# Releasing the Q, K and V loads of later batches one attention unit at a time, and moving two other loads to another DMA queue

## The chip, the cores and the metric

The kernel runs on one core of a Trainium2 chip. The metric is the device time of one execution in microseconds (us). On the chips used here the kernel before varied from 345 to 350 us in nearly all of its runs, so differences under 1% are not read as effects.

## The reference, cut to what matters

```python
# attention: 8 batches, 8 heads, 576 positions, head size 64, window of 32 on each side
scores = scale * q @ k.T ;  masked outside |i - j| <= 32 ;  softmax ;  x = attn @ v
# then, on all 4608 tokens (x is 4608 x 512):
h = x @ w_in                  # 512 -> 2048
g = s * max(h, 0)**2 + b      # s and b are two scalars
out = g @ w_out               # 2048 -> 512
```

## The kernel before

The kernel is written as a list of tasks. Each has an engine, a function, an assumed duration, and what it reads and writes. A small scheduler in Python orders the tasks per engine by simulating them with the assumed durations, including the DMA transfers. On the chip, each engine then executes its own list strictly in that order and waits on semaphores. So an assumed duration is never waited for. It only decides the order, and an engine whose next instruction is not ready stands still even if a later one is ready.

The parts that matter here, with cuts marked `...`:

```python
add("pool", [lambda e: e.dma_start(SB128[:, 0:1], moe_s.partition_broadcast(128)),      # s, b by GpSimd
             lambda e: e.dma_start(SB128[:, 1:2], moe_b.partition_broadcast(128))], ...)

def load_v(b, h, key, stream, waits=()):      # V of one head -> VST; stream is the issuing engine
    ...
def cast_v(b, key, engines, slack):           # VST (f32) -> VBD (bf16), on VectorE and ScalarE
    ...
def chunk(b, t0, n, key):                     # one of three pieces of Q and of K, b >= 2
    for name in "qk":
        add("sp", ... dma_start(STG ...),
            waits=[land["av", b - 1, {0: int(b > 3), 256: 2, 512: 3}[t0]]], ...)
        add("dve", ... NAT <- STG ...)        # cast
        add("sp", ... QT or KT <- NAT, transpose=True ...)
    ...
def unit(b, m):                               # one of five attention units of a batch
    ...   # scores, exp, AV, normalise; XT <- XN by a DMA transpose from SP for b >= 2
    land["av", b, m] = g.tasks[-1]            # the AV matmuls: what later loads wait for
...
# batch 1
    w_out(0); qk(1, 0, 128)
    for h in range(H):
        load_v(1, h, nxt(), "pool", waits=[land["out", 2, 0]])
    cast_v(1, due(1, 0) - 4.0, (("dve", "act"), ("dve", "act")), 800.0)
...
# batches 2 to 7
    for h in range(H):
        load_v(b, h, due(b, 0) - 30.0 + 0.1 * h, "pool", waits=[land["av", b - 1, 1]])
```

`land["av", b - 1, u]` is the end of the AV matmuls of unit `u` of the batch before. VST is a single buffer, filled in 8 pieces of 144 KB for batches 0 and 1, and 16 of 72 KB later. Plain loads, the DMA transposes of xt, Q and K, and the output DMAs are all issued by SP. V of batches 1 to 7 and the scalars are issued by GpSimd (POOL).

The softmax here doesn't subtract the row's maximum and nothing guards it: scores larger than these inputs give would overflow.

## Time and profile before

The median was 347.02 us (346.45 to 349.16, three runs). The profiled run spans 345.8 us.

First, lines of the profile page of the kernel before: busy time with its share of the span, and then the span in 40 equal slices, with busy tenths, the granted TensorE clock in tenths and the DMA share in tenths.

```profile
PE 311.9 (90%) x2234; PEld 178.4 (52%) x2234; DVE 208.0 (60%) x485; ACT 167.2 (48%) x270; POOL 95.5 (28%) x146
...
PE   1587948997999998799979998999999999999995
...
PEclk9999987999999999899999999999999999999999
DMA  6999996799799699936994799569942111110021
```

TensorE (PE) is busy 90% of the time and is the bound. DMA is saturated for the first 50 us, then comes in bursts. The clock drops twice, each time behind a gap in the PE row.

The windows view of the kernel before gives, for each stretch, its length and then PE, PEld, DVE, ACT and POOL busy with their counts, the granted clock, the DMA share and GB/s.

```profile
0.00:20.00 20.00, 7.58 (x62) 5.33 (x62) 11.95 (x28) 12.92 (x16) 13.96 (x29) 1.00 0.94 209
20.00:40.00 20.00, 16.59 (x236) 14.19 (x237) 11.37 (x25) 13.08 (x25) 9.18 (x11) 1.00 1.07 346
40.00:60.00 20.00, 13.96 (x152) 11.74 (x151) 11.85 (x18) 10.97 (x17) 11.90 (x12) 0.83 0.96 228
60.00:80.00 20.00, 20.00 (x228) 16.92 (x226) 10.11 (x23) 10.09 (x21) 10.58 (x17) 1.00 0.93 201
80.00:130.00 50.00, 48.23 (x356) 27.34 (x355) 41.09 (x105) 30.18 (x49) 18.29 (x29) 1.00 0.94 187
130.00:180.00 50.00, 44.83 (x270) 22.50 (x269) 31.95 (x76) 22.73 (x36) 11.70 (x20) 0.97 0.94 183
```

The idle time of TensorE in a stretch is its length less PE busy: 12.4 us in the first 20 us, 6.0 us between 40 and 60, 5.2 us between 130 and 180. The clock of 0.83 over 20 us stands for 6.8 us at half rate. The same view with narrower stretches:

```profile
49.70:53.40 3.70, 0.00 (x0) 0.00 (x0) 3.01 (x6) 2.15 (x4) 0.00 (x0) 0.50 1.12 278
53.40:56.60 3.20, 3.20 (x18) 2.28 (x19) 3.20 (x6) 1.82 (x2) 2.63 (x2) 0.51 1.02 336
141.90:145.30 3.40, 3.40 (x10) 1.22 (x8) 3.40 (x6) 1.30 (x3) 0.00 (x0) 0.50 1.16 233
```

The view of waits for PE of the kernel before has who waited for whom, the total, how often, and the longest.

```profile
...
PE o L715 <- DVE gt L705: 5.8, 1, 5.8
PE w L696 <- DMA xt<-xn: 4.3, 2, 2.2
PE o L474 <- DVE nat L470: 2.9, 1, 2.9
...
PE o L715 <- DVE outs L728: 1.6, 1, 1.6
```

The 5.8 us are at 47.6 to 53.4 us, the 4.3 us are two waits for transposes of xt between 130 and 180 us, and the 2.9 us are in the startup. The timelines of VectorE and GpSimd show what lies behind the first one (start, duration, engine, line, operation; in brackets the idle time before it and what ended it).

```profile
50.39 1.42 DVE L447 CAST vbd<-vst 64x1024 bf16<-64x1024 f32 x2 [5.86 <-DMA vst<-in_v_dram]
...
36.96 5.89 POOL L433 DMA_DIRECT2D vst<-in_v_dram  x8 [0.73 <-DMA stg<-in_moe_w_out_dram]
48.65 1.04 POOL L466 CAST nat<-stg 128x1024 bf16<-128x1024 f32 x1 [3.21 <-DMA stg<-in_q_dram]
53.91 1.68 POOL L466 CAST nat<-stg 32x1024 bf16<-32x1024 f32 x1 [4.22 <-DMA stg<-in_q_dram]
```

VectorE stands 5.86 us in front of the cast of V of batch 1, and the gt tile that TensorE wants comes after that cast in VectorE's list.

### The profile page before, as it was taken

How to read it: one execution, taken by the hardware profiler on the slowest of the kernel's cores; microseconds unless marked ns; L12 is line 12 of the kernel's file. 1: busy time of each engine (PE TensorE's matmuls, PEld its weight loads, DVE VectorE, ACT ScalarE, POOL GpSimd, SP SyncE). 2: the span in 40 equal slices, each digit the busy share in tenths (PEclk: the TensorE clock that was granted, in tenths of full speed). 3: DMA queues.
4: the chain of work that ended last, by engine and by line, in shares of the span. 5: the costliest groups of instructions: out<-in, count | busy, mean ns of one | idle time of the engine just before them, and what ended most of it. 6: DMA issues, size and time to landing. Idle time of an engine off the chain costs nothing.

```text
span 345.8 us, 5858 instructions
## 1 busy us (share of the span) xinstructions
PE 311.9 (90%) x2234; PEld 178.4 (52%) x2234; DVE 208.0 (60%) x485; ACT 167.2 (48%) x270; POOL 95.5 (28%) x146
## 2 busy tenths in 40 slices
PE   1587948997999998799979998999999999999995
PEld 0456846884564564255535554555455544444442
DVE  6565538646985984587567666964984453333321
ACT  6596537635662763365337446544654433333300
POOL 7652836470290082006400640074000000000000
PEclk9999987999999999899999999999999999999999
DMA  6999996799799699936994799569942111110021
GB/s 189 219 342 363 264 226 209 191 226 193 168 245 204 152 166 210 217 106 165 230 196 121 189 209 220 151 162 231 223 105 76 47 46 44 40 51 32 30 78 75
DMA packets 103388, 57.15 MB, mean 165 GB/s; under 512 B 51776, under 2 KB 95424, under 8 KB 103360
## 3 DMA queue, kind: packets, MB, share of 16 engines
q1 hardware_dynamic: 98176, 48.51, 61.0%
q0 software_dynamic: 5184, 8.27, 12.2%
q8 instruction: 17, 0.28, 0.3%
q14 instruction: 11, 0.09, 0.1%
HBM read 36.70 MB, written 9.44 MB: 133 GB/s over the span
## 4 chain that ended last, share of the span: by engine, by line
PE 58%; DMA 28%; SPq 5%; DVE 3%; POOL 3%; issue 1%; ACT 0%; DVEq 0%; POOLq 0%
PE o L715 25%; PE w L696 25%; DMA xt<-xn 10%; DMA stg<-in_k_dram 7%; DMA vst<-in_v_dram 5%; PE avn L583 4%; DMA stg<-in_moe_w_in_dram 3%; PE sc L544 3%; DMA stg<-in_q_dram 3%; SPq L433 3%; POOL vst L433 3%; SPq L457 1%; SPq L417 1%; DVE vbd L447 1%; DVE nat L507 1%
## 5 line engine op out<-in xcount | busy, mean ns | idle before, releaser
L715 PE MATMUL o<-wout,gt 128*128 128x512 bf16 (+1 forms) x640 | 143.5, 359 | 7.8 <-DVE gt L705 5.8
L696 PE MATMUL w<-xt,win 128*128 128x512 bf16 (+2 forms) x704 | 145.7, 344 | 4.3 <-DMA xt<-xn 4.3
L703 ACT ACTIVATE r<-w 128x512 bf16<-128x512 f32 x144 | 85.6, 597 | 104.9 <-PE w L696 91.7
L433 POOL DMA_DIRECT2D vst<-in_v_dram x104 | 65.9, 641 | 117.3 <-PE avn L583 111.5
L705 DVE TENSOR_TENSOR gt<-r 128x512 bf16<-128x512 bf16 x144 | 62.2, 438 | 57.3 <-ACT r L703 56.7
L715 PEld LDWEIGHTS o<-wout,gt 128*128 128x128 bf16 x640 | 61.2, 98 | 66.6 <-DVE gt L705 6.3
L696 PEld LDWEIGHTS w<-xt,win 128*128 128x128 bf16 x704 | 62.1, 99 | 58.0 <-DMA xt<-xn 5.2
L728 DVE SCALAR_TENSOR_TENSOR outs<-o,sb,cvec 128x512 f32<-128x512 f32 (+1 forms) x40 | 27.7, 692 | 17.1 <-PE o L715 17.0
L561 ACT ACTIVATE exe<-sc 128x512 bf16<-128x512 f32 (+1 forms) x40 | 27.6, 690 | 11.9 <-PE sc L544 11.8
L583 PE MATMUL avn<-vbd,exo 128*128 128x130 bf16 (+1 forms) x240 | 27.7, 220 | 4.5 <-ACT xt L608 2.2
L596 DVE TENSOR_TENSOR xn<-avn,rec 128x512 bf16<-128x512 f32 (+1 forms) x38 | 26.1, 686 | 9.1 <-DMA xt<-xn 8.5
L446 ACT CAST vbd<-vst 64x1024 bf16<-64x1024 f32 (+1 forms) x15 | 16.6, 1140 | 24.2 <-DMA vst<-in_v_dram 24.2
L507 DVE CAST nat<-stg 128x1024 bf16<-128x1024 f32 (+1 forms) x36 | 24.2, 683 | 4.0 <-DMA stg<-in_q_dram 2.8
L583 PEld LDWEIGHTS avn<-vbd,exo 128*128 128x128 bf16 (+1 forms) x240 | 21.7, 104 | 9.2 <-ACT xt L608 2.4
L583 PE MATMUL avn<-vbd,exe 128*128 128x130 bf16 (+1 forms) x152 | 25.1, 219 | 0.5 <-ACT vbd L446 0.5
L561 ACT ACTIVATE exo<-sc 128x512 bf16<-128x512 f32 x32 | 23.7, 741 | 3.4 <-PE sc L544 3.4
L544 PEld LDWEIGHTS sc<-qt,kbd 128*128 128x128 bf16 x288 | 20.3, 100 | 9.6 <-issue 0.9
L544 PE MATMUL sc<-qt,kbd 128*128 128x128 bf16 (+1 forms) x288 | 24.7, 220 | 0.1
L447 DVE CAST vbd<-vst 64x1024 bf16<-64x1024 f32 (+1 forms) x16 | 11.6, 747 | 14.6 <-DMA vst<-in_v_dram 14.6
L522 DVE COPY kbd<-kt 64x512 bf16<-64x512 bf16 (+1 forms) x72 | 18.3, 254 | 0.9
L583 PEld LDWEIGHTS avn<-vbd,exe 128*128 128x128 bf16 (+1 forms) x152 | 16.0, 108 | 3.6 <-ACT vbd L446 0.6
L565 DVE TENSOR_TENSOR exe<-exe,mask 128x512 bf16<-128x512 bf16 (+1 forms) x30 | 11.8, 392 | 5.9 <-ACT exe L561 5.4
(65 smaller groups left out, 135.6 us busy)
## 6 DMA issues: line engine op xcount, KB each, us to landing
stg<-in_q_dram SPq DMA_DIRECT2D x16, 512.0 KB, 5.1
stg<-in_k_dram SPq DMA_DIRECT2D x16, 512.0 KB, 8.3
out_dram<-outs SPq DMA_DIRECT2D x32, 256.0 KB, 2.2
vst<-in_v_dram POOLq DMA_DIRECT2D x96, 72.0 KB, 7.4
stg<-in_moe_w_in_dram SPq DMA_DIRECT2D x8, 512.0 KB, 9.2
stg<-in_moe_w_out_dram SPq DMA_DIRECT2D x8, 512.0 KB, 11.2
vst<-in_v_dram SPq DMA_DIRECT2D x8, 144.0 KB, 4.6
vst<-in_v_dram POOLq DMA_DIRECT2D x8, 144.0 KB, 8.4
```

What stands on the lines that cost most here:

```text
L433: add(stream, lambda e, dst=dst, src=src: e.dma_start(dst, src), 640.0 if stream == "sp" else 700.0, writes=[("VST", h, x) for x in (range ...
L507: add("dve", lambda e, si=si, ni=ni: e.tensor_copy(NAT[ni][0:n, :, :].rearrange("p i (h d) -> p h i d", h=H), STG[si][0:n, 0:1024].rearran ...
L522: add("dve", lambda e, i=i, p0=p0: e.tensor_copy(KBD[p0:p0 + 64, :, j0:j0 + nj, p0 + 32 * i:p0 + 32 * i + 32], KT[p0:p0 + 64, i, :, t0 // ...
L544: fns = [lambda e, j=j, pr=pr, lo=lo, hi=hi, w=w, par=par: e.matmul(SC[:, par, pr * 128:pr * 128 + w], lhsT=KBD[:, pr, j, :], rhs=QT[slot] ...
L561: add("act", lambda e, src=src, dst=dst: e.activation(dst.rearrange("p a (c i) -> p a i c", i=2), src, AF.Exp, bias=0.0, scale=0.125), 190 ...
L583: fns.append(lambda e, pr=pr, buf=buf, col=col, j=j, x=x, last=len(parts) - 1: e.matmul(av[0:nr, pr, 0:130], lhsT=buf[:, pr, col:col + nr] ...
L596: add("dve", lambda e: e.tensor_tensor(XN[xi][0:nr, :].rearrange("p (a b c) -> p a b c", a=4, b=2), av[0:nr, :, 0:128].rearrange("p a (b c ...
L696: add("pe", [lambda e, g=g, kc=kc: e.matmul(wt[:, g, :], lhsT=WIN_BF[:, kc, (f0 + g) * 128:(f0 + g + 1) * 128], rhs=XT[:, kc, t0 % XR:t0 % ...
L703: add("act", lambda e: e.activation(rt, wt, AF.Relu, bias=0.0, scale=1.0), 190 + 0.833 * 512, reads=[("W", wb)], writes=[("R1", rb)], key=key)
L705: add("dve", lambda e: e.tensor_tensor(GT[gs][:, f0:f0 + ng, g0:g0 + nt], rt, rt, ALU.mult), 130 + 0.53 * 512, reads=[("R1", rb)], writes= ...
L715: add("pe", [lambda e, fc=fc: e.matmul(O[:, ob, 0:cn], lhsT=GT[gs][:, fc, g0:g0 + 128], rhs=WOUT_BF[:, fc, c0:c0 + cn], start=(fc == 0), s ...
L728: add("dve", lambda e: e.scalar_tensor_tensor(OUTS[us][:, 0:cn], O[:, ob, 0:cn], SB128[:, 0:1], CVEC[:, c0:c0 + cn], ALU.mult, ALU.add), 2 ...
```

## The change

The intent: load V of batch 1 and the two scalars through SP; let each Q, K and V piece of batches 2 to 7 follow its own attention unit of the batch before, instead of several following one unit; and bring the scheduler's assumed durations nearer to measured ones. The core of the diff:

```diff
+XTS = 4000.0
+PACE = ((0, 0, 1, 2, 3, 3), (0, 0, 1, 2, 3, 3), (0, 1, 2, 3, 3, 3))
+PACEV = ((0, 0, 1, 1), (0, 0, 1, 1), (0, 1, 2, 2))
-        add("pool", [lambda e: e.dma_start(SB128[:, 0:1], moe_s.partition_broadcast(128)),
-                     lambda e: e.dma_start(SB128[:, 1:2], moe_b.partition_broadcast(128))], ...
+            for i, src in enumerate((moe_s, moe_b)):          # after the w_in loads
+                add("sp", lambda e, i=i, src=src: e.dma_start(SB128[:, i:i + 1], src.partition_broadcast(128)), ...
-                load_v(1, h, nxt(), "pool", waits=[land["out", 2, 0]])
+                load_v(1, h, nxt(), "sp", waits=[land["out", 2, 0]])
-                    load_v(b, h, due(b, 0) - 30.0 + 0.1 * h, "pool", waits=[land["av", b - 1, 1]])
+                    load_v(b, h, due(b, 0) - 30.0 + 0.1 * h, "pool", waits=[land["av", b - 1, PACEV[min(b, 4) - 2][h // 2]]])
-                    waits=[land["av", b - 1, {0: int(b > 3), 256: 2, 512: 3}[t0]]], dma=("l", n // 2, 28.5))
+                    waits=[land["av", b - 1, PACE[min(b, 4) - 2][t0 // 128 + "qk".index(name)]]], dma=("l", n // 2, 30.0))
 # assumed durations (they only order the instructions); two lines that sum up seven edits
-  w_out DMA 46.0, weight casts dve 650 / pool 1500, V DMA pool 230 / sp 20, Q K DMA 27.4, Q cast pool 1400
+  w_out DMA 48.0, weight casts dve 690 / pool 1100, V DMA pool 370 / sp 21, Q K DMA 30.0, Q cast pool 1150
-                writes=[("W", wb)], key=key, slack=1500.0)    # first matmuls behind a DMA transpose
+                writes=[("W", wb)], key=key, slack=XTS)
```

No arithmetic and no bytes change. Because the scheduler reruns, the order of the instructions on every engine changes too.

## The prediction

> **What bounds the kernel now.** TensorE does. The page's busy table has PE at 311.9 of 345.8 us. The windows view (10 us stretches) places the 34 us of idle: about 20 us before 40 us, where inputs and weights arrive (DMA share 1.05 to 1.13); 6.0 us between 40 and 60; about 8.3 us between 80 and 250; then none until the last few microseconds. After 250 us PE never stops. Two steps of the granted clock go with the stalls: the 50 to 60 us window has 0.67 and the 140 to 150 us window 0.83, which cost about 3.3 and 1.7 us. This fits the Trainium skill, "TensorE: Matmul & The Clock Gate", Part 1: an idle array falls to half rate. So about 19 us sit in stalls after 40 us.
>
> **What they are.**
> 1. 47.6 to 53.4 us: PE waits 5.84 us for a gt tile of VectorE. In the timeline, VectorE stands in order behind the cast of V of batch 1, which waits 5.86 us until V lands at 50.4. GpSimd issued that V from 37.0 to 42.8 (734 ns each, 8.4 us median to landing), into a saturated DMA system.
> 2. 83 us: PE waits 1.6 us behind VectorE, which waited for V of batch 2 (16 issues, 65.4 to 75.4; last landing at 81.2).
> 3. 130 to 180 us: PE waits 2.2 and 2.0 us for DMA transposes of xt, which took about 9 us where the median is 2.6. All 16 V pieces are released by one attention unit and issued in 10 us among Q and K pieces of 512 KB: DMA share 1.1 to 1.2, then 0.2 to 0.6.
> 4. 211 and 246 us: 0.9 and 0.4 us behind K loads that took 12 to 14 us.
>
> **What the change does.** No arithmetic and no bytes change. The second batch's V goes from the GpSimd queue into SP's, in order with the Q, K loads. An SP issue of V took 1.17 us for batch 0 (8 in 9.34 us), so it costs SP about 3 us more, but V no longer shares with Q and K pieces issued after it. I estimate its landing at 48 to 49 us instead of 50.4, and the later Q, K about 2 us later. The s and b loads leave GpSimd (1.3 us, not critical). In the steady part V is released by two or three units in turn, and Q and K one unit apart: bursts become a flatter load, so transposes and K loads should lose most of their waiting. The larger assumed DMA times and the 4.0 us allowance behind transposes order consumers later.
>
> **Sum.** Stall 1 with its clock loss: 9.2 us, of which I expect 5 (what follows it is still fed by DMA; new waits for Q or K appear). Stall 2: 1 of 1.6. Stalls 3 and 4 with the clock loss and small gaps: 4 of 8. Startup: 0. About 9.5 us less: 337.5 us, range 332 to 344. Faster by over 2%: 0.72; within: 0.25; slower: 0.03.
>
> **What would show it.** PE idle from 40 to 60 us below 3 us, and a clock near 1.0 there; no xt wait over 1 us between 130 and 180; peak DMA share nearer 1.0; PE busy near 307 us (less half-rate time); the idle before 40 us and the tail unchanged.
>
> **What would make it wrong.** VectorE still blocks on V of batch 1, as SP's slow issue lands it later than the schedule believes; SP's in-order waits for attention units hold up the transposes and outputs behind them; or the new order of instructions opens stalls in the startup.

## The result, and the profile after

| | before | after |
|---|---|---|
| time, median (range), 4 runs each | 348.09 us (346.45 to 349.35) | 333.11 us (331.69 to 334.12) |
| ratio, 95% interval | | 0.9569 (0.9508 to 0.963) |
| span of the profiled run | 345.8 us | 331.1 us |
| TensorE busy | 311.9 us | 308.5 us |

Ratios here are the mean time of one kernel's fast runs over that of the other's in the same rounds, so not quite the ratio of the medians quoted.

The profile page of the kernel after, the same rows:

```profile
PE 308.5 (93%) x2199; PEld 179.5 (54%) x2234; DVE 206.6 (62%) x485; ACT 166.4 (50%) x270; POOL 87.6 (26%) x136
...
PE   1778998899999999999989999999999999999995
...
PEclk9999999799999999999999999999999999999999
DMA  8999999899999699979998996999811111000021
```

Most of the holes in the middle of the PE row are gone. The windows view of the kernel after:

```profile
0.00:20.00 20.00, 9.50 (x80) 6.86 (x82) 11.87 (x29) 14.45 (x19) 14.50 (x28) 1.00 1.07 238
20.00:40.00 20.00, 17.60 (x252) 16.04 (x250) 12.96 (x27) 12.86 (x24) 7.19 (x7) 1.00 1.10 343
40.00:60.00 20.00, 17.76 (x212) 15.35 (x213) 11.57 (x24) 15.35 (x28) 8.36 (x9) 1.00 1.11 254
60.00:80.00 20.00, 18.84 (x172) 14.38 (x171) 12.38 (x27) 9.05 (x15) 8.17 (x14) 0.92 0.95 213
80.00:130.00 50.00, 49.63 (x349) 27.66 (x354) 39.07 (x100) 27.73 (x47) 19.82 (x32) 1.00 1.10 194
130.00:180.00 50.00, 48.79 (x318) 25.86 (x322) 38.45 (x93) 26.72 (x43) 14.05 (x23) 1.00 1.04 203
```

From these and the later stretches of the same view comes a ledger of TensorE's idle time (length less busy):

| stretch, us | idle before | idle after | gain |
|---|---|---|---|
| 0 to 20 | 12.42 | 10.50 | 1.92 |
| 20 to 40 | 3.41 | 2.40 | 1.01 |
| 40 to 80 | 6.04 | 3.40 | 2.64 |
| 80 to 130 | 1.77 | 0.37 | 1.40 |
| 130 to 180 | 5.17 | 1.21 | 3.96 |
| 180 to 250 | 1.37 | 0.65 | 0.72 |
| from 250 | 3.78 | 4.07 | -0.29 |
| all | 33.96 | 22.60 | 11.36 |

The other 3.3 us are in TensorE's busy time (311.9 less 308.5). Half rate explains about half of them. Before, it cost 3.3 us (above). After, one stretch of half rate is left, at 60.0 us; TensorE was busy throughout it, and it cost 1.7 us.

```profile
60.00:63.40 3.40, 3.40 (x21) 2.58 (x19) 0.36 (x1) 0.61 (x1) 3.09 (x6) 0.50 1.04 271
```

So 1.6 us are the clock's, and the remaining 1.8 us are not explained. The trace after lacks 35 of 2234 matmul records; its busy time may be too low for that reason, and its idle time too high by as much.

The waits of PE in the kernel after:

```profile
...
PE o L717 <- DVE outs L730: 1.3, 1, 1.3
...
PE w L698 <- ACT r L705: 1.2, 2, 0.9
...
PE o L473 <- DVE nat L469: 1.1, 1, 1.1
```

The wait for gt and both waits for xt are gone. The next lines, from the timelines of VectorE, GpSimd and SP after, answer those shown of before.

```profile
43.45 1.45 DVE L469 CAST nat<-stg 128x1024 bf16<-128x1024 f32 x2 [0.21 <-DMA stg<-in_k_dram]
52.38 1.42 DVE L446 CAST vbd<-vst 64x1024 bf16<-64x1024 f32 x2 [1.16 <-DMA vst<-in_v_dram]
...
45.06 1.42 POOL L465 CAST nat<-stg 32x1024 bf16<-32x1024 f32 x1 [2.48 <-DMA stg<-in_q_dram]
...
40.62 8.75 SPq L432 DMA_DIRECT2D vst<-in_v_dram  x8
```

V of batch 1 now lands **later**, at 52.4 us instead of 50.4. What came earlier are Q and K: the last Q cast starts at 45.1 us instead of 53.9. SP put V behind them in its queue (40.6 to 49.4 us).

The transposes of xt did not get faster on the whole, but the longest ones, for which TensorE had waited, are gone. These lines of the view of the tile xt from 120 to 250 us give the time from issue to landing, before and then after:

```profile
DMA to landing us min/median/max: 2.3/4.7/13.4
```

```profile
DMA to landing us min/median/max: 2.3/5.7/7.9
```

The median of all 32 rose from 2.6 to 5.7 us, but it mixes in the quick transposes after 250 us, when few loads are left. From 80 to 120 us, single ones after still took 8 to 11 us (at most 7.4 before), and TensorE did not wait for them.

### The profile page after: what moved, and what is told of

It reads as the page before. It is cut to its first block, busy times and chain, and to the rows that moved or that the text cites. A ratio compares the mean times of both kernels' runs of the same rounds, so it can differ in the third digit from the quotient of the medians.

```text
span 331.1 us, 5839 instructions
## 1 busy us (share of the span) xinstructions
PE 308.5 (93%) x2199; PEld 179.5 (54%) x2234; DVE 206.6 (62%) x485; ACT 166.4 (50%) x270; POOL 87.6 (26%) x136
## 3 DMA queue, kind: packets, MB, share of 16 engines
q0 software_dynamic: 4608, 7.08, 11.3%
## 4 chain that ended last, share of the span: by engine, by line
PE 70%; DMA 13%; SPq 8%; POOL 3%; DVE 2%; ACT 2%; issue 2%; ACTq 0%
PE o L717 31%; PE w L698 29%; PE avn L582 6%; SPq L432 5%; DMA vst<-in_v_dram 5%; PE sc L543 3%; DMA stg<-in_moe_w_in_dram 3%; DMA stg<-in_moe_w_out_dram 3%; POOL vst L432 2%; SPq L456 2%; DMA out_dram<-outs 2%; ACT vbd L445 1%; SPq L416 1%; PE o L740 1%; DVE vbd L446 0%
## 5 line engine op out<-in xcount | busy, mean ns | idle before, releaser
L717 PE MATMUL o<-wout,gt 128*128 128x512 bf16 (+1 forms) x629 | 140.4, 357 | 1.9 <-DVE outs L730 1.3
L698 PE MATMUL w<-xt,win 128*128 128x512 bf16 (+2 forms) x685 | 139.8, 339 | 2.2 <-ACT r L705 1.2
L707 DVE TENSOR_TENSOR gt<-r 128x512 bf16<-128x512 bf16 x144 | 61.3, 432 | 55.1 <-ACT r L705 54.4
L698 PEld LDWEIGHTS w<-xt,win 128*128 128x128 bf16 x704 | 61.6, 98 | 52.4 <-ACT r L705 1.8
L432 POOL DMA_DIRECT2D vst<-in_v_dram x96 | 59.4, 626 | 106.8 <-PE avn L582 57.7
L521 DVE COPY kbd<-kt 64x512 bf16<-64x512 bf16 (+1 forms) x72 | 19.1, 266 | 0.8
L446 DVE CAST vbd<-vst 64x1024 bf16<-64x1024 f32 (+1 forms) x16 | 11.7, 745 | 7.3 <-DMA vst<-in_v_dram 7.3
L564 DVE TENSOR_TENSOR exe<-exe,mask 128x512 bf16<-128x512 bf16 (+1 forms) x30 | 11.7, 391 | 7.1 <-ACT exe L560 7.0
```

The source lines that it names most:

```text
L432: add(stream, lambda e, dst=dst, src=src: e.dma_start(dst, src), 640.0 if stream == "sp" else 700.0, writes=[("VST", h, x) for x in (range ...
L698: add("pe", [lambda e, g=g, kc=kc: e.matmul(wt[:, g, :], lhsT=WIN_BF[:, kc, (f0 + g) * 128:(f0 + g + 1) * 128], rhs=XT[:, kc, t0 % XR:t0 % ...
L707: add("dve", lambda e: e.tensor_tensor(GT[gs][:, f0:f0 + ng, g0:g0 + nt], rt, rt, ALU.mult), 130 + 0.53 * 512, reads=[("R1", rb)], writes= ...
L717: add("pe", [lambda e, fc=fc: e.matmul(O[:, ob, 0:cn], lhsT=GT[gs][:, fc, g0:g0 + 128], rhs=WOUT_BF[:, fc, c0:c0 + cn], start=(fc == 0), s ...
```

## The experiments

Three questions were put to the chip. Is it the traffic itself (which loads are in flight together) or only the new order of instructions? What is each part worth? What does the startup owe to it?

The scheduler reorders everything at each edit, so simple one-part edits mix a part's effect with reordering. Six experiments therefore **freeze the order**: they plan with the unchanged kernel and edit a queue, a release or a buffer only after planning. Comparing the instruction listings confirmed that in all six the order on TensorE, VectorE and ScalarE is that of the kernel they start from.

| run | base | median, us | ratio to before (95%) |
|---|---|---|---|
| f_before_spread | before, frozen | 338.14 | 0.9732 (0.9681 to 0.9783) |
| f_before_early | before, frozen | 344.60 | 0.9900 (0.9866 to 0.9935) |
| f_before_v1sp | before, frozen | 356.25 | 1.0252 (1.0199 to 1.0305) |
| f_after_burst | after, frozen | 338.59 | 0.9733 (0.9671 to 0.9796) |
| f_after_v1pool | after, frozen | 338.76 | 0.9760 (0.9690 to 0.9829) |
| f_out5 | after, frozen | 333.68 | 0.9575 (0.9526 to 0.9625) |
| a_pace | before, rescheduled | 342.04 | 0.9839 (0.9780 to 0.9897) |
| a_costs | before, rescheduled | 347.19 | 0.9974 (0.9907 to 1.0042) |
| a_v1sb | before, rescheduled | 340.53 | 0.9780 (0.9696 to 0.9865) |
| a_cast_late | before, rescheduled | 349.22 | 1.0064 (1.0008 to 1.0120) |
| l_costs | after, rescheduled | 338.16 | 0.9714 (0.9662 to 0.9766) |
| l_qk | after, rescheduled | 339.43 | 0.9740 (0.9686 to 0.9793) |

The kernel before ran beside every experiment; the kernel after did not, so differences to it come from medians of different sessions (the ratios to the kernel before give 5 to 7 us where the text says 5 to 6). All gave correct results, with three timed rounds and one profile each. The medians of f_after_burst, a_pace, a_costs, a_v1sb and f_out5 include one slow run each; the ratios do not.

### f_before_spread: only the release of V changes

```diff
 g.plan()
+for b, vs in VL.items():            # V pieces of batches 2..7; order of all else as planned
+    for t, h in vs: the wait for unit 1  ->  unit PACEV[min(b, 4) - 2][h // 2] of batch b - 1
```

> The kernel before, with the order of every instruction on TensorE, VectorE, ScalarE and SP kept as it was; only the V pieces of batches 2 to 7 are released by two or three attention units in turn (as after) instead of by one. Theory T (traffic: the flatter DMA load is what helps): the xt waits of 2.2 and 2.0 us and the half-rate clock behind them go, 341 to 343 us against 347 to 348. Theory O (order: what helps is where the schedule puts each instruction in the in-order streams): within 1%, 345 us or more.

Measured: 338.14 us, 9 to 10 us less, with not one compute instruction moved. Its view of waits has this line for xt:

```profile
PE w L699 <- DMA xt<-xn: 0.6, 1, 0.6
```

The idle time between 80 and 250 us fell from 8.31 to 1.65 us, and the clock between 130 and 180 us is 1.00. The gain is larger than T's range (341 to 343 us) has it. O is refuted for the steady part: it is when V's loads are in flight that matters, not the order of the compute instructions. Whether it is the flatter load, as T has it, is the next question.

### f_before_early: still one burst, one unit earlier

```diff
 g.plan()
+for b, vs in VL.items():
+    for t, h in vs: the wait for unit 1  ->  unit 0 of batch b - 1   (all 16 pieces)
```

> The kernel before, same order of compute instructions and of SP; all V pieces of batches 2 to 7 still in one burst, but released one unit earlier (by unit 0 of the batch before). Theory E (earlier release is what helped in f_before_spread, since V lands before its cast): as fast as f_before_spread, 337 to 340 us, stalls at 83 us and for xt gone. Theory S (spreading is what helped): the stall at 83 us goes (about 2 us), but xt transposes still wait 2 us each behind the burst; 344 to 346 us.

Measured: 344.60 us. The total falls where S put it, but the trace contradicts S: no wait for xt over 0.5 us is left, and the idle time between 80 and 250 us is 1.74 us, as good as with spreading. What it loses is elsewhere, and belongs to this edit. GpSimd executes in order, and all 16 issues of batch 2's V now stand in its list before the last cast of w_out:

```profile
60.51 10.39 POOL L434 DMA_DIRECT2D vst<-in_v_dram  x16
70.89 1.05 POOL L421 CAST wout<-stg 128x1024 bf16<-128x1024 f32 x1
```

```profile
PE o L741 <- POOL wout L421: 5.6, 2, 5.4
```

(The first fence is its timeline of GpSimd, the second its waits of PE.) This wait and the half rate behind it (a clock of 0.83 from 60 to 80 us) are of the size of the 6.5 us between this run and f_before_spread. So it is not shown that spreading is better than an earlier burst. Both cure the steady part. In the kernel before, the burst of V is released by unit 1, which for batches 4 to 7 is also the unit that releases Q and K of the next batch; both cures break that up. Which of the overlaps hurt most was not separated.

### f_after_burst: the burst put back into the kernel after

```diff
 g.plan()
+for b, vs in VL.items():
+    for t, h in vs: the waits for units PACEV  ->  unit 1 of batch b - 1   (all 16 pieces)
```

> The kernel after, same order of compute instructions and of SP; only the V pieces of batches 2 to 7 are released in one burst by unit 1 of the batch before, as in the kernel before. T: waits for transposes of xt come back, 337 us or more against 333. O: within 1% of after, 332 to 335 us (ratio to before about 0.96).

Measured: 337.67 to 339.14 us in its three fast runs, about 5 us over the kernel after. The total is T's. Its profiled run was a slow one (342.94 us), so its trace is read with care: it leaves only 0.23 us of idle time between 130 and 250 us, hence no xt waits. Its losses lie earlier: a wait of 3.5 us for an output buffer at 57 to 61 us (1.3 us in the kernel after), and batch 2's V, released at 67.3 us instead of 55.5 and waited for at about 83 us. In the order of the kernel after, then, the later batches bear a burst in that trace, and the late start for batch 2 is what the burst can be seen to cost there. This rests on the one slow run, so what the 5 us of the fast runs consist of is not shown.

### f_before_v1sp and f_after_v1pool: only the queue of batch 1's V changes

```diff
 g.plan()
+for t in V1: t.stream, t.dma = "sp", ("l", 36, 21.0)        # f_before_v1sp
+for t in V1: t.stream, t.dma = "pool", ("v", 1.125, 370.0)  # f_after_v1pool
```

> The kernel before, same order of compute instructions; only the eight V pieces of batch 1 go through SP's queue instead of GpSimd's. T: V lands before 50.4 us, VectorE blocks 3 us or less (5.86 before), the time falls to about 343 us. O: VectorE still stands behind the cast of V, which lands no earlier, and later Q and K are delayed; 347 us or more.

Measured: 356.25 us, slower by 2.5% (2.0 to 3.1%). Here SP's list has V between the w_out loads, and V comes last:

```profile
56.09 1.42 DVE L450 CAST vbd<-vst 64x1024 bf16<-64x1024 f32 x2 [13.52 <-DMA vst<-in_v_dram]
```

VectorE's old list needs V early, so it stands 13.5 us, and TensorE 12.4 us behind it. Meanwhile the last Q cast starts at 47.2 us instead of 53.9. Neither theory had both: Q and K came earlier, and V later.

> The kernel after, same order of compute instructions; only the V pieces of batch 1 go back to GpSimd's queue. T: a stall of 3 us or more in TensorE between 45 and 60 us, 336 us or more. O: V lands no later than the 52.3 us of the kernel after, 331 to 335 us.

Measured: 338.76 us, about 5.5 us over the kernel after. Q and K come late again (VectorE, then GpSimd, in the timelines; after, the same casts start at 43.5 and 45.1 us):

```profile
49.46 0.69 DVE L472 CAST nat<-stg 128x1024 bf16<-128x1024 f32 x1 [3.84 <-DMA stg<-in_k_dram]
51.95 0.68 DVE L472 CAST nat<-stg 32x1024 bf16<-32x1024 f32 x1 [1.79 <-DMA stg<-in_k_dram]
...
52.81 1.39 POOL L468 CAST nat<-stg 32x1024 bf16<-32x1024 f32 x1 [7.46 <-DMA stg<-in_q_dram]
```

The two runs, each with its compute order frozen, show what the move to SP does in this saturated stretch. It gives the DMA time to Q and K first and to V last: Q and K come 6 to 8 us earlier in both pairs, and V about 6 us later in the first (its cast starts at 56.1 instead of 50.4 us). The move is worth about 5.5 us if the compute lists want Q and K first, and costs over 8 us if they want V first. The Trainium skill, "DMA: Bandwidth & Descriptors", "Issuing engines are not separate DMA queues", says that DMAs of all issuing engines run on the same 16 DMA engines and interleave. The trace agrees: V issued by GpSimd delays SP's Q and K by 6 to 8 us.

### a_cast_late: one assumed number

```diff
-cast_v(1, due(1, 0) - 4.0, (("dve", "act"), ("dve", "act")), 800.0)
+cast_v(1, due(1, 0) - 4.0, (("dve", "act"), ("dve", "act")), 6000.0)
```

> The kernel before with one number changed: the cast of V of batch 1 is scheduled as if V came 5.2 us later (allowance 6000 ns instead of 800). Nothing moves between queues. O: VectorE no longer blocks behind that cast, the 5.84 us stall of TensorE and its half-rate clock go, 338 to 342 us. T: V is what TensorE waits for, the stall moves to a later instruction and the time stays at 346 us or more.

Measured: 349.22 us, no gain. VectorE no longer stands before V's cast. It stands before K's instead:

```profile
53.53 1.49 DVE L470 CAST nat<-stg 128x1024 bf16<-128x1024 f32 x2 [5.58 <-DMA stg<-in_k_dram]
```

So this other order does not cure the 5.8 us stall. With V on GpSimd, V and the last pieces of Q and K are cast only from 50 us on (53.5 and 55.0 us for K and Q here), and whatever the list asks for first is waited for.

### a_pace, a_costs, a_v1sb: one part alone, rescheduled

The edits are the matching hunks of the diff above: PACE and PACEV; the assumed durations with XTS; V of batch 1 and the scalars on SP.

> The kernel before with the new release of Q, K and V alone (old assumed durations, V of batch 1 and scalars on GpSimd), rescheduled. T: most of the steady gain, 338 to 342 us. O (the assumed durations carry it): 344 us or more; the stall at 47 to 53 us stays in both.

> The kernel before with the new assumed durations and the longer allowance behind transposes alone, rescheduled; no DMA queue or release changes. O: 340 us or less, with the 5.8 us stall for VectorE gone or under 2 us. T: 345 us or more.

> The kernel before with only the loads of V of batch 1 and of the scalars moved to SP, rescheduled. T: the stall at 47 to 53 us under 3 us, and 1 to 2 us less idle TensorE before 20 us; 340 to 343 us. O: the startup gain alone, 345 to 347 us.

Measured: 342.04, 347.19 and 340.53 us. The releases and the two queue moves gain 1.6% and 2.2% on their own; the durations gain nothing. a_pace keeps the 5.7 us wait for gt at 47 to 53 us, as expected. a_v1sb has no idle time at all between 40 and 60 us (V's cast starts at 49.8 us there; SP issues no w_out load in front of V), but still 3.6 us of waits for xt between 125 and 185 us. The two parts cure different stalls. a_pace has the same release of V as the frozen f_before_spread and yet is 3 to 4 us slower; what differs is the release of Q and K and a new order, which this pair doesn't separate.

### l_costs and l_qk: the change without one part, rescheduled

l_costs keeps the old assumed durations and the allowance of 1.5 us; l_qk keeps the old waits of `chunk` (both pieces of a chunk wait for one unit).

> The kernel after with the old assumed durations and the old allowance of 1.5 us behind transposes, rescheduled: only queues and releases as in the change. If the durations matter only through chance reordering (a_costs gave nothing): 331 to 337 us. If the new releases need them: 338 us or more, with xt waits back between 130 and 180 us.

> The kernel after with the old release of Q and K (both of a chunk by one unit), the new release of V kept, rescheduled. If V's release is the whole effect of the pacing: 331 to 335 us. If Q and K's matters too: 336 us or more, with TensorE idle between 80 and 250 us up from 2.2 us to 5 or more.

Measured: 338.16 and 339.43 us, both about 5 to 6 us over the kernel after. l_costs has the total of the second reading but not its reason: the loss is not through xt, since its idle time between 130 and 180 us is 0.37 us. It loses 7.5 us of idle time between 60 and 130 us, for an exp tile (2.9 us) and for K of batch 2 (2.7 us). l_qk has 6.7 us idle between 80 and 250 us instead of 2.2, as the second reading said. Both kernels have other instruction orders than the kernel after, so how much of each loss is the part itself and how much a less lucky order stays open.

### f_out5: a try to improve

The chain of waits of the kernel after has one 6.86 us piece of an output DMA queued behind weight loads. Five output buffers instead of three, order frozen:

> A try to improve on the kernel after: same order of every instruction, but five output buffers instead of three, so that VectorE does not wait for output DMAs that queue behind weight loads at 51 to 58 us (a 6.86 us wait in the chain). If that wait is what leaves TensorE idle 2.2 us at 40 to 60 us and at half rate for 3.4 us after: 329 to 331 us. If TensorE waits for V or the weights there anyway: 332 to 334 us.

Measured: 332.68, 332.87 and 334.49 us, against 331.69 to 334.12 for the kernel after: no gain. The piece in the chain was not what limited it. The other, profiled run took 816.5 us, with correct results; its matmuls of 512 columns took about 0.6 us each (26 in 15.46 us in its chain of waits, where 4 took 0.86 us otherwise), so its trace says nothing of this edit. No experiment beat the kernel after.

### The startup

No run was made for the startup alone, but all traces split in two. With the scalars on GpSimd (the kernel before and six experiments) TensorE idles 11.7 to 12.8 us in the first 20 us; with them on SP (the kernel after, a_v1sb, l_costs, l_qk, f_after_burst, f_after_v1pool) 9.4 to 10.9 us. Without the two scalar DMAs at its head, GpSimd does a 2 us memset of VBD at 0.8 us. With them, that memset starts at 7.47 us, just before VectorE's first cast of K. VectorE and GpSimd in the kernel before, and then in the kernel after:

```profile
8.22 1.81 DVE L470 CAST nat<-stg 128x1024 bf16<-128x1024 f32 x1 [0.72 <-DMA stg<-in_k_dram]
...
7.47 2.01 POOL L336 MEMSET vbd<- 64x2304 bf16 x1
```

```profile
7.45 0.68 DVE L469 CAST nat<-stg 128x1024 bf16<-128x1024 f32 x1
...
0.81 2.01 POOL L339 MEMSET vbd<- 64x2304 bf16 x1 [0.29 <-POOLq L827]
```

The cast ends 0.55 us after the memset does (10.03 against 9.48 us). The Trainium skill, "SBUF — State Buffer", "SBUF: two separate sides", says that GpSimd and those VectorE operations that use two ports share a port pair as an exclusive lock: whichever starts first has it for its whole instruction. The traces agree, in both directions. In a_costs the cast came first (7.41 us) and took 0.68 us, and the memset stretched instead:

```profile
7.41 0.68 DVE L470 CAST nat<-stg 128x1024 bf16<-128x1024 f32 x1
10.44 0.35 DVE L383 COPY mask<-mask 128x384 bf16<-128x384 bf16 x1 [2.35 <-POOL mask L347]
...
7.47 2.57 POOL L336 MEMSET vbd<- 64x2304 bf16 x1
```

(The profiled run of a_costs was a slow one, 350.12 us; these are single instructions of its first 11 us, and its 11.7 us of startup idle time is used with that caution.) The clash itself is the smaller part of the loss. After the memset GpSimd makes the last mask, and VectorE copies it. That copy starts at 10.44 us in a_costs, where the cast was quick, and at nearly the same time in the kernel before, but earlier in the kernel after:

```profile
10.22 0.35 DVE L383 COPY mask<-mask 128x384 bf16<-128x384 bf16 x1 [0.18 <-POOL mask L347]
```

```profile
8.62 0.35 DVE L386 COPY mask<-mask 128x384 bf16<-128x384 bf16 x1 [0.49 <-POOL mask L350]
```

VectorE's next copies, of K to kbd, start at 11.16 us before, 10.71 in a_costs and 9.25 after. A quick cast alone thus brings kbd about 0.4 us, and the mask about 1.5 us more; the mask is late because the memset stands before it in GpSimd's list. This is read from three traces; no run moved the memset alone. The rest of the startup gain was not taken apart.

## Why the prediction was right or wrong

The time was predicted right: 333.11 us lies inside 332 to 344, and the change is faster by over 2%. The estimate of 337.5 us was 4.4 us too high. Point by point:

- **What bounds the kernel: right. The pool of about 19 us in stalls after 40 us: 1.7 us too large.** The 3.3 us of clock loss that it has for 50 to 60 us count time at half rate in which TensorE stood idle, so that time is counted twice; 1.6 us fell on busy time. After 40 us the gain is 8.4 us of idle time, 1.6 us of half rate and the 1.8 us that are not explained.
- **Stall 1: half the expected gain, and the mechanism wrong.** Expected was 5 of 9.2 us. Measured for 40 to 80 us: 2.6 us of idle time and nothing of clock (1.6 us before, 1.7 after, only later), so 2.5 us. And the step "I estimate its landing at 48 to 49 us instead of 50.4, and the later Q, K about 2 us later" was wrong on both counts. V landed at 52.4 us and the last Q some 9 us earlier. f_before_v1sp shows that V on SP in the old order is a loss; a_cast_late shows that a later cast alone cures nothing. The gain needs both the queue and a schedule that asks for Q and K first.
- **Stall 2: right.** Expected 1 of 1.6 us; the stretch 80 to 130 us lost 1.4 us of idle time.
- **Stalls 3 and 4: cause right, size too small.** Expected 4 of 8 us. Measured: 4.7 us of idle time between 130 and 250 us and 1.7 us of clock, 6.4 us. f_before_spread shows the cause, the release of V, with the order frozen.
- **"Bursts become a flatter load, so transposes and K loads should lose most of their waiting": half right.** The load is no flatter by the measure that the prediction named: the DMA share peaks at 1.32 in the 10 us windows, against 1.22 before. The typical transpose is not faster either. But between 120 and 250 us the longest fell from 13.4 to 7.9 us, and TensorE's waits for them went. In f_before_spread these waits went too, although its longest transpose there still took 11.3 us. So shorter transposes are not the only way, and two other reasons stay possible: V out of the way at the right time (f_before_spread, f_before_early), and an order with more room behind the transposes (f_after_burst, one slow trace).
- **Startup 0: wrong.** It gave 2.9 us before 40 us, of which 1.9 in the first 20 us go with the scalars' queue. "The s and b loads leave GpSimd (1.3 us, not critical)" looked at the 1.3 us of issuing and not at where the memset then stands in GpSimd's list. This is the largest single part of the missed 4.4 us; stalls 3 and 4 add 2.4.
- **The half-rate clock: the link is right, the cost was counted too high** (first point). The Trainium skill, "TensorE: Matmul & The Clock Gate", Part 1, says that an idle array falls to half rate, and the traces agree: behind the wait that ended at 141.56 us in the kernel before, 8 matmuls took 3.34 us, later 1.73 us. The clock is 1.00 between 40 and 60 us and between 130 and 180 us in the kernel after, and where the stalls return in an experiment, low clock returns with them (0.76 between 40 and 60 us in f_before_v1sp). The wait need not be long: before the half rate at 60.0 us in the kernel after, the longest was 1.34 us, ending at 58.8 us.

In part the good total is luck: stall 1 brought 2.5 us less than expected, and a startup gain of 2.9 us that was put at 0 made up for it.

## What to carry to other kernels

In the saturated stretch here, moving a load to another queue decided which load arrived first (Q and K 6 to 8 us earlier, V later). So change the queue and the order of the consumers together and check which of the loads the consumers ask for first. In a self-ordering kernel, freeze the order and edit only a queue or a release: that separated an effect of 2.7% from reordering, where rescheduled edits left it ambiguous. Read the trace even when the total agrees with a theory: one run here had the predicted time for a reason the trace refuted. And count low clock as a loss only where TensorE is busy.

## What the Trainium skill lacked or had wrong

- "DMA: Bandwidth & Descriptors", "Issuing engines are not separate DMA queues", says that issuing from several engines only saves issue time. Here the issuing queue of 1.18 MB of V, with every compute instruction in the same order, changed the time by +2.5% (f_before_v1sp) or by about 5.5 us (f_after_v1pool against after). The section does not mention that the queue also sets the order of arrival; how the engines take turns between queues is under another heading of that page, without a figure for what it is worth to a kernel.
- The same page does not say how differently the two paths cut the same transfer. Moving the 8 V pieces (144 KB each, rows of 256 bytes) from GpSimd to SP took 512 packets from the software queue (5184 to 4672) and added 4736 to the hardware queue (98176 to 102912), in f_before_v1sp against before: 64 packets for each piece against 592. Issuing one of them took GpSimd 0.73 us and SP 0.61 to 2.16 us.
- "SBUF — State Buffer", "SBUF: two separate sides", was right: 1.81 instead of 0.68 us for a VectorE cast behind a GpSimd memset, and 2.57 instead of 2.01 us for the memset behind the cast.
- "TensorE: Matmul & The Clock Gate" has half rate and other low-rate states, and a warning that trace records of the clock can be unreliable. One run here (f_out5, 816.5 us) had matmuls at about 0.6 us instead of 0.216 us, 0.36 of the full rate, with a granted clock of 1.00 in its record throughout. The page mentions slow matmuls of about that length, but no state of 0.36, and the runs do not explain it.
